# Three of four later taps of a causal convolution as a ScalarE product and a GpSimd add, in a fused attention-and-gate kernel on one core

## The chip, the cores and the metric

The kernel runs on one core of one Trainium2 chip. The metric is the device time of one execution in microseconds; the time before the change is the median of three runs, 591.73 us (590.05 to 592.37). Five engines work side by side, each through a queue of its own in the order in which the program gives it instructions: TensorE (PE, with its weight loads PEld), VectorE (DVE), ScalarE (ACT), GpSimd (POOL), and SyncE (SP), which here only issues DMAs. An engine whose next instruction waits for a semaphore holds up all that stands behind it in its queue.

## What is computed

Sigmoid attention over 8 batches of 12 heads, its result laid out as 768 features per token; then a gate (a causal convolution of five taps along the tokens, and a sigmoid), a product with `w_val`, the gate times that, and a product with `w_out`.

```python
def _attn_ref(q, k, v):                     # (8, 12, 448, 64) each
    scores = scale * np.matmul(q, k.transpose(0, 1, 3, 2)) - np.log(S)
    attn = 1.0 / (1.0 + np.exp(-scores))
    return np.matmul(attn, v).astype(np.float32)

def _moe_ref(x, w_val, conv_w, w_out):      # x: (8, 448, 768)
    xp = np.concatenate([np.zeros((B, K - 1, D), dtype=np.float32), x], axis=1)
    for k in range(K):                      # K = 5
        gate_pre += conv_w[k][None, None, :] * xp[:, k:k + S, :]
    gate = 1.0 / (1.0 + np.exp(-gate_pre))
    val = x @ w_val
    return (gate * val @ w_out).astype(np.float32)
```

## The kernel before

**Units.** Two heads make a pair (48, index `i`), two pairs a double pair (24, index `j`), three double pairs a batch. For a pair PE makes the scores of three chunks of 128 keys (`scores`, L496); the 64 keys that are left over are done for both pairs of a double pair at once (`scores_rest`, L518). ACT applies the sigmoid to each chunk (`attention`, L531). `attend` (L581, L589) multiplies with v into a bank of PSUM, and `after` copies that to `x`.

**Plain and split float32.** A plain pair multiplies float32 by float32 directly (`qk_single`, `a_single`). A split pair replaces each operand by a high and a low part and adds three faster products: `qk_hi` by a copy (L355 on DVE or L353 on ACT) and `qk_lo` by a subtraction on POOL (L364); `a` by a scaled copy on ACT (L359) and a DVE subtraction (L542), and `v_hi`, `v_lo`. `WHOLE_SCORES` lists the pairs with plain scores, `WHOLE` the double pairs with a plain attend.

**Convolution and products.** The first batch's attention output is cut into seven slices, one of which goes to each other batch: so seven batches of 512 tokens pass through gate and products. In `after`, for each of a double pair's two blocks of 128 features, the first tap is a scaled copy on ACT or DVE, and the four later taps are each one DVE instruction, `gate = x * w + gate` (L645); then ACT applies the sigmoid to the gate (L648). `x_scale` finds a batch's scale (with a small matmul, L665), `x_split` makes `xs` (L688), its high and low part. `product` (L707) makes one block of 128 output features from 18 matmuls of 512 columns: six blocks of input times three terms. The `val` products are taken out of PSUM by DVE (L717) and multiplied with the gate, the `out` products by ACT or DVE (`scaled`, L359 or L361), and go to the output in two DMAs (L725, L726). PSUM has three buffers for attention (`ps_a`) and two for products (`ps_m`).

**What sets the order.** Each piece of work is recorded by `op` with the engines that may do it, an assumed cost for each, a due time, and the buffers that it reads and writes. `Plan.issue` then simulates the engines once, before the program is built, and gives every engine the ready piece that is due first; a piece with two possible engines goes to the one that comes free. The due times come from the table `AT` and from `tau(i)`, which counts 8.2 for each of the first 12 pairs and 11.51 for the later ones. The plan keeps DVE and POOL from running together where both of their instructions carry `port="VG"`. Since the order is fixed when the program is built, a change of `AT` or of an assumed cost moves instructions in every queue.

**First loads.** A pair's q and k are one DMA of 896 columns (`load`, L459), v is one per double pair (`load_v`, L463), each weight column one of 768 KB (L402), all issued by SP.

## Time and profile before

| | |
|---|---|
| median of three runs | 591.73 us (590.05 to 592.37) |
| the profiled execution | 592.33 us; its span 590.5 us |
| instructions in the span | 9085 |
| bytes moved by DMA | 56.94 MB, 28.7% of the 16 DMA engines' span |
| granted TensorE clock | 1.00 throughout |

The profile is of one execution. Its page gives for each engine the time in which it worked, and a chain of waits followed back from the last instruction. Matmuls overlap: one of 512 columns is recorded with 379 ns, but the next begins 216 ns behind it. So a busy PE is best read by the distance from the start of one piece of work to the start of the next, in the timeline. The stages of the span are: loads until about 4 us; attention alone, with the conversion of the weights on DVE and ACT, until about 104 us; attention and products interleaved until about 500 us; and the last twelve products, some with nothing left beside them.

### The profile page before, as it was taken

To read this page: it belongs to the slowest core of one execution; us is meant where nothing else is said; L and a number is where in the kernel's file an instruction comes from. 1 tells how busy PE (TensorE), PEld (TensorE's weight loads), DVE (VectorE), ACT (ScalarE), POOL (GpSimd) and SP (SyncE) were. 2 spreads that over 40 slices of the span, in tenths; PEclk is the share of its full clock that TensorE was granted. 3 is DMA by queue.
4 is the path that set the end of the run, shared out by engine and by line. 5 is a ranking of instruction groups with operands and counts; after the bars stand their busy time and mean duration, and the time that the engine had idled before them with its cause. 6 is when DMAs were issued, how large, how long until landed. Compare 5 with 4: busy or idle time off the path is not lost. (4 is left out here: it accounts for less than half of the span.)

```text
span 590.5 us, 9085 instructions
## 1 busy us (share of the span) xinstructions
PE 578.1 (98%) x3503; PEld 273.4 (46%) x3503; DVE 463.4 (78%) x766; ACT 366.9 (62%) x478; POOL 70.5 (12%) x88
## 2 busy tenths in 40 slices
PE   8999999999999999999999999999999999999996
PEld 4333334444555445454454545545544455444442
DVE  0889999989999998989989899897982998722210
ACT  5678768566786767767776677676653875421111
POOL 0000202122111031111211111110011200000000
PEclk9999999999999999999999999999999999999999
DMA  8978622240423023231141411324004110021012
GB/s 322 382 276 275 223 95 65 66 117 18 130 72 109 11 84 130 81 101 62 32 130 47 134 63 33 99 72 139 1 34 158 37 42 1 1 71 37 1 36 72
DMA packets 30523, 56.94 MB, mean 96 GB/s; under 512 B 13968, under 2 KB 19344, under 8 KB 30480
## 3 DMA queue, kind: packets, MB, share of 16 engines
q1 hardware_dynamic: 30480, 56.37, 28.7%
q8 instruction: 27, 0.44, 0.3%
q14 instruction: 16, 0.13, 0.1%
HBM read 43.96 MB, written 12.40 MB: 95 GB/s over the span
## 5 line engine op out<-in xcount | busy, mean ns | idle before, releaser
L707 PE MATMUL ps_m<-g,w_out_hi 128*128 128x512 f16 x504 | 150.0, 379 | 1.3 <-ACT y L359 0.9
L707 PE MATMUL ps_m<-xs,w_val_hi 128*128 128x512 f16 x504 | 150.1, 379 | 0.6 <-DVE y L717 0.4
L645 DVE SCALAR_TENSOR_TENSOR gate<-x,cw,gate 128x512 f32<-128x512 f32 x168 | 121.8, 753 | 0.8
L364 POOL TENSOR_TENSOR qk_lo<-qk_src,qk_hi 128x448 fp32r<-128x448 f32 (+1 forms) x56 | 64.7, 1171 | 300.5 <-DVE qk_hi L355 111.3
L707 PE MATMUL ps_m<-xs,w_val_lo 128*128 128x512 f16 x252 | 95.5, 379 | 0.0
L707 PE MATMUL ps_m<-g,w_out_lo 128*128 128x512 f16 x252 | 95.5, 379 | 0.0
L542 DVE SCALAR_TENSOR_TENSOR a<-ps_a,a 128x896 f16<-128x896 f32 x84 | 89.0, 1082 | 4.8 <-ACT a L359 4.5
L531 ACT ACTIVATE ps_a<-ps_a 128x896 f32<-128x896 f32 x98 | 86.7, 906 | 8.6 <-DVE v_exp L523 7.8
L707 PEld LDWEIGHTS <-w_val_hi 128*128 128x128 f16 x504 | 47.9, 98 | 62.8 <-issue 7.8
L707 PEld LDWEIGHTS <-w_out_hi 128*128 128x128 f16 x504 | 48.0, 98 | 61.6 <-issue 6.3
L359 ACT ACTIVATE a<-ps_a 128x896 f16<-128x896 f32 x84 | 74.5, 924 | 0.3
L531 ACT ACTIVATE a_single<-ps_a 128x896 f32<-128x896 f32 x70 | 60.0, 922 | 7.2 <-PE ps_a L496 4.7
L359 ACT ACTIVATE y<-ps_m,o_scale 128x512 f32<-128x512 f32 x38 | 25.5, 686 | 60.6 <-PE ps_m L707 53.8
L717 DVE SCALAR_TENSOR_TENSOR y<-ps_m,y_scale,gate 128x512 f32<-128x512 f32 x42 | 29.9, 745 | 33.5 <-PE ps_m L707 33.5
L496 PE MATMUL ps_a<-qk_single 64*128 64x448 f32 x240 | 51.1, 555 | 2.2 <-DMA qk_single<-qk 1.4
L353 ACT CAST g<-y 128x512 f16<-128x512 f32 x33 | 20.5, 620 | 52.6 <-DVE y L717 52.2
L589 PE MATMUL ps_a<-a_single,v_src 128*64 128x448 f32 x240 | 47.3, 543 | 0.0
L589 PE MATMUL ps_a<-a,v_hi 128*64 128x448 f16 x336 | 46.1, 354 | 0.0
L648 ACT ACTIVATE gate<-gate 128x512 f32<-128x512 f32 x42 | 26.0, 627 | 28.9 <-DVE gate L645 28.7
L707 PEld LDWEIGHTS <-w_val_lo 128*128 128x128 f16 x252 | 24.7, 98 | 29.7
L707 PEld LDWEIGHTS <-w_out_lo 128*128 128x128 f16 x252 | 24.6, 98 | 29.8
L359 ACT ACTIVATE gate<-x,cw 128x512 f32<-128x512 f32 x32 | 23.1, 735 | 20.1 <-DVE y L717 20.1
(104 smaller groups left out, 658.4 us busy)
## 6 DMA issues: line engine op xcount, KB each, us to landing
qk_src<-qk SPq DMA_DIRECT2D x28, 448.0 KB, 3.7
v_src<-vs SPq DMA_DIRECT2D x24, 448.0 KB, 3.4
out_t<-y SPq DMA_DIRECT2D x42, 224.0 KB, 2.0
qk_single<-qk SPq DMA_DIRECT2D x20, 448.0 KB, 6.1
w_words<-w_val SPq DMA_DIRECT2D x6, 768.0 KB, 9.7
w_words<-w_out SPq DMA_DIRECT2D x6, 768.0 KB, 6.0
x<-first_x SPq DMA_DIRECT2D x21, 68.0 KB, 2.3
first_x<-x_first SPq DMA_DIRECT2D x3, 452.0 KB, 7.1
```

The costliest lines, as they stand in the source:

```text
L353: nc.scalar.copy(to, x)
L359: nc.scalar.activation(to, x, AF.Copy, scale=by)
L364: engines[eng].tensor_tensor(to, x, y, op=ALU.subtract)
L496: mm(b()[:, h, :S], k()[rows, at : at + P], q()[rows, :S], start=(n == 0), stop=(n == len(terms(i)) - 1))
L531: nc.scalar.activation(to, b()[:, :, :S], AF.Sigmoid, bias=-math.log(S), scale=1.0 / math.sqrt(D))
L542: op({"V": 1.0}, t + 0.5, lambda e: nc.vector.scalar_tensor_tensor(part(1), p(), A_SCALE, part(0), op0=ALU.mult, op1=ALU.subtract), [b], [ ...
L589: mm(px()[to, p, :S], v()[:, o : o + D], x(st[2 * j + p]["a", c])[:, h, at : at + S], start=False, stop=(c == 2 and n == len(parts) - 1), ...
L645: op({"V": 0.67}, at + AT["tap_step"] * k, lambda e, p=p, g=g, w=w, k=k: nc.vector.scalar_tensor_tensor(by(g()), x()[:, p, :, HALO - k : H ...
L648: op({"A": 0.55}, t + AT["gate"] + AT["tap_pair"] * p, lambda e, g=g: nc.scalar.activation(g(), g(), AF.Sigmoid), [], [g])
L707: mm(po(), w()[:, c, :], x(k), start=(c == 0 and j == 0), stop=(c == NC - 1 and j == 2))
L717: op({"V": 0.6}, t + AT["y"], lambda e: nc.vector.scalar_tensor_tensor(y(), po(), y_scale()[:, m : m + 1], gate(), op0=ALU.mult, op1=ALU.m ...
```

## The change

**The taps.** From the second batch on, three of the four later taps (`ADDED`; one of four in the first that has a gate, `ADDED_FIRST`) are no longer one DVE instruction each: ACT makes the product of `x` and the tap's weight into a new buffer, of which there are two (`tap_ring`), and POOL adds it to the gate. That is 114 of the 168.

```diff
-EARLY = 6
+EARLY = 5
+ADDED_FIRST = 1
+ADDED = 3
...
+    tap_ring = ring(sb, 2, [P, T], F32, "tap")
...
             for k in range(1, KT):
+                if k > KT - 1 - (ADDED_FIRST if f == 1 else ADDED):
+                    tap = tap_ring.new()
+                    op({"A": 0.61}, at + AT["tap_step"] * k - AT["tap_first"], lambda e, p=p, w=w, k=k, tap=tap: scaled(
+                        e, by(tap()), x()[:, p, :, HALO - k : HALO + SL - k], w(k)), [x, own, edge, cw], [tap])
+                    op({"G": 1.27}, at + AT["tap_step"] * k, lambda e, g=g, tap=tap: nc.gpsimd.tensor_tensor(
+                        g(), g(), tap(), op=ALU.add), [tap], [g])
+                    continue
                 op({"V": 0.67}, at + AT["tap_step"] * k, lambda e, p=p, g=g, w=w, k=k: nc.vector.scalar_tensor_tensor(
```

**Plain pairs.** Twenty pairs with plain scores become sixteen, ten double pairs with a plain attend nine.

```diff
-WHOLE = {*range(9), 21}
-WHOLE_SCORES = {*range(15), 17, 24, 39, 42, 43}
+WHOLE = {*range(8), 10}
+WHOLE_SCORES = {*range(15), 17}
```

**The first loads** get due times of their own, in the order of the pairs, and the very first is cut into 576 and 320 columns; chunk 0 of pair 0 waits only for the former.

```diff
+        x, t = s["qk"], t + AT["load_qk_first" if i < AHEAD else "load_qk"] if i >= 4 else -1e3 + i
+        if i:
+            op({"S": 0.45}, t, lambda e: nc.sync.dma_start(x(), qk[i]), [], [x], P * QW * 4)
+            return
+
+        s["more"] = more = x.part()
+        for n, (b, cs) in enumerate(((x, slice(0, S + P)), (more, slice(S + P, QW)))):
+            op({"S": 0.45}, t + 0.5 * n, lambda e, cs=cs: nc.sync.dma_start(
+                x()[:, cs], qk[i][:, cs]), [], [b], P * (cs.stop - cs.start) * 4)
...
-        op({"S": 0.45}, tau(2 * j) + AT["load_v"], lambda e: nc.sync.dma_start(v(), vs[j]), [], [v], P * VW * 4)
+        op({"S": 0.45}, tau(2 * j) + AT["load_v"] if j else -990, lambda e: nc.sync.dma_start(v(), vs[j]), [], [v], P * VW * 4)
...
-    def sources(i):
+    def sources(i, c=None):
+        if i == 0 and c != 0:
+            return [st[i]["qk"], st[i]["more"]]
```

SP's queue at the start of the program; `qk_single` is a pair's q and k, `v_src` a double pair's v. Before:

```order
L459 DMA qk_single_149<-qk 128x896
L463 DMA v_src_155<-vs 128x896
L459 DMA qk_single_157<-qk 128x896
L459 DMA qk_single_159<-qk 128x896
L463 DMA v_src_161<-vs 128x896
L459 DMA qk_single_163<-qk 128x896
L459 DMA qk_single_165<-qk 128x896
L402 DMA w_words_167<-w_val 128x768
```

SP's queue at the same place now:

```order
L471 DMA qk_single_149<-qk 128x576
L471 DMA qk_single_149<-qk 128x320
L466 DMA qk_single_156<-qk 128x896
L466 DMA qk_single_158<-qk 128x896
L466 DMA qk_single_160<-qk 128x896
L476 DMA v_src_162<-vs 128x896
L476 DMA v_src_164<-vs 128x896
L407 DMA w_words_166<-w_val 128x768
```

Both v loads stand behind four pairs; the first weight stands behind six loads' worth of bytes where there were seven.

**The last product** (block 5 of the last batch's `out`) is made as two of 256 columns, each with its own `ps_m` bank, eviction and DMA.

```diff
+        if (n, b, m) == ("out", B - 1, NC - 1):
+
+            y = y_ring.new()
+            for k, (low, cs) in enumerate(((y, slice(0, T // 2)), (y.part(), slice(T // 2, T)))):
+                po = columns(cs, t + k * STEP / 4)
+                op({"A": 0.35, "V": 0.4}, t + k * STEP / 4 + AT["o"], lambda e, cs=cs, po=po: scaled(
+                    e, y()[:, cs], po()[:, cs], outer[b]()[:, m : m + 1]), [po, outer[b]], [low], port="")
+                cs = slice(cs.start, min(cs.stop, S))
+                op({"S": 0.45}, t + k, lambda e, cs=cs: nc.sync.dma_start(out[b, m, :, cs], y()[:, cs]), [low], [], P * 1000)
+            op({"S": 0.45}, t + 2, lambda e: nc.sync.dma_start(out[0, m, :, S - SL :], y()[:, S:]), [low], [], P * 1000)
+            return
+        po = columns(slice(0, T), t)
```

`columns` holds the loop of 18 matmuls that stood in `product`, over a slice of columns.

**Due times and assumed costs.** Nearly every entry of `AT` has a new number, and some assumed costs too (POOL's 1.27 for `g_lo` is 1.17). Two entries:

```diff
-    first=8.2, step=11.51, val=-64.5, val_step=38.05, out=-42, out_step=46.57, w_max=-113, w_split=-46.5,
+    first=8.4, step=14.21, val=-51.5, val_step=42.5, out=-27, out_step=35.57, w_max=-84.5, w_split=-74,
```

What that moves on PE is seen where the first product begins. Before, behind the scores of pair 15 (the last row of `qk_lo` in each list is the last term of a chunk; the pair's first chunks are left out here):

```order
L496 MATMUL ps_a<-qk_lo,qk_hi 128x448 x2
L414 LDWEIGHTS ones
L414 MATMUL ps_m<-out_max,ones 128x1
L665 LDWEIGHTS ones
L665 MATMUL ps_m<-diagonal,ones 128x128
L518 MATMUL ps_a<-qk_src 64x448 x2
L518 MATMUL ps_a<-qk_single 64x448 x2
L581 MATMUL ps_a<-a_single,v_src 64x448 x4
L589 MATMUL ps_a<-a_single,v_src 64x448 x12
L496 MATMUL ps_a<-qk_hi 128x448 x2
L496 MATMUL ps_a<-qk_hi,qk_lo 128x448 x2
L496 MATMUL ps_a<-qk_lo,qk_hi 128x448 x2
```

Two more chunks of pair 16 follow there, and then the first product. PE's queue now, at the end of the same pair 15:

```order
L511 MATMUL ps_a<-qk_hi 128x448 x2
L511 MATMUL ps_a<-qk_hi,qk_lo 128x448 x2
L511 MATMUL ps_a<-qk_lo,qk_hi 128x448 x2
L731 LDWEIGHTS w_val_hi_73
L731 MATMUL ps_m<-xs,w_val_hi_73 128x512
```

The first product now stands directly behind pair 15; the rest, the attend and pair 16 come after the first two products.

In the middle of the program, ACT's queue (numbers tell the tiles apart; `tap` is the new buffer, `x` the convolution's input, `ps_a` a chunk of scores in PSUM). Before:

```order
L359 ACTIVATE a_2897<-ps_a_2852 128x2x448
L359 ACTIVATE gate_2907<-x_2465,cw_68 128x512
L359 ACTIVATE gate_2912<-x_2465,cw_68 128x512
L353 CAST g_2941<-y_2930 128x512
L531 ACTIVATE ps_a_2932<-ps_a_2932 128x2x448
L531 ACTIVATE ps_a_2943<-ps_a_2943 128x2x448
```

ACT's queue now, at the same double pair's first taps:

```order
L364 ACTIVATE tap_3033<-x_2565,cw_68 128x512
L364 ACTIVATE a_3039<-ps_a_2977 128x2x448
L364 ACTIVATE tap_3046<-x_2565,cw_68 128x512
L364 ACTIVATE tap_3062<-x_2565,cw_68 128x512
L364 ACTIVATE tap_3076<-x_2565,cw_68 128x512
L546 ACTIVATE ps_a_3066<-ps_a_3066 128x2x448
```

Two first taps stood between the scaled copy of one pair and the sigmoids of the next; now four products of later taps do, and the third and fourth of them need a buffer that POOL's add must have read before the sigmoid behind them can start.

## What is predicted

> **What bounds the kernel now.** I read the page's busy shares first, then the stages, then what TensorE waited for.
>
> ```profile
> PE 578.1 (98%) x3503; PEld 273.4 (46%) x3503; DVE 463.4 (78%) x766; ACT 366.9 (62%) x478; POOL 70.5 (12%) x88
> ```
>
> TensorE (PE) is busy for 98% of the span. The table of stages shows where the others stand (PE, weight loads, DVE, ACT, POOL, each with its busy us):
>
> ```profile
> 0.00:15.00 15.00, 12.23 (x86) 6.76 (x88) 0.76 (x3) 8.33 (x10) 0.89 (x11) 1.00 0.85 323
> 15.00:100.00 85.00, 82.37 (x475) 31.27 (x473) 79.72 (x160) 64.32 (x80) 6.72 (x7) 1.00 0.65 227
> 100.00:400.00 300.00, 299.45 (x1917) 149.15 (x1917) 277.65 (x440) 212.38 (x280) 52.43 (x59) 1.00 0.25 79
> ```
>
> From 100 to 400 us VectorE (DVE) is at 277.65/300 = 93%, ScalarE (ACT) at 71%, GpSimd (POOL) at 17%, and PE stands still for 0.55 us in all. DVE is nearly full but has not been the bound. A kernel like this gets faster by less PE work or by fewer PE waits. The waits are short; the longest three and the shortest of ten:
>
> ```profile
> PE ps_a L496 <- DMA qk_single<-qk: 1.4, 1, 1.4
> PE ps_m L707 <- ACT y L359: 1.1, 3, 0.8
> PE ps_m L740 <- DVE ones L733: 1.1, 1, 1.1
> ...
> PE ps_a L496 <- ACT a_single L531: 0.3, 1, 0.3
> ```
>
> All ten add up to 7.5 us; without the DMA row and the row of the warm-up's `ones`, 5.0 us are left that ACT and DVE could give back. So the relief of DVE, the largest part of the change in instructions, can be worth 5 us at the very most, and nothing for certain.
>
> **Plain or split pairs: less PE work.** `WHOLE_SCORES` goes from 20 pairs to 16, `WHOLE` from 10 double pairs to 9. The timeline of PE gives the price of each unit from the start of one piece to the start of the next. First a plain pair of scores and a plain attend:
>
> ```profile
> 111.94 2.53 PE L496 MATMUL ps_a<-qk_single 64*128 64x448 f32 x12
> 114.40 0.60 PE L707 MATMUL ps_m<-xs,w_val_hi 128*128 128x512 f16 x2
> ...
> 123.08 0.93 PE L581 MATMUL ps_a<-a_single,v_src 64*64 64x448 f32 x8
> 128.60 0.47 PE L496 MATMUL ps_a<-qk_hi 64*128 64x448 f32 x2
> ```
>
> Then the same in split form:
>
> ```profile
> 248.19 0.17 PE L515 MATMUL ps_a<-vm,ones 128*128 128x1 bf16 x1
> 248.28 0.98 PE L518 MATMUL ps_a<-qk_src 64*64 64x448 f32 x8
> 249.09 0.56 PE L581 MATMUL ps_a<-a_rest,v_hi 64*64 64x448 f16 x8
> ...
> 253.29 0.47 PE L496 MATMUL ps_a<-qk_hi 64*128 64x448 f32 x2
> ...
> 255.31 0.60 PE L707 MATMUL ps_m<-xs,w_val_hi 128*128 128x512 f16 x2
> ```
>
> Plain scores take 114.40 - 111.94 = 2.46 us, split ones 255.31 - 253.29 = 2.02: 0.44 less, four times, 1.76. A plain attend takes 128.60 - 123.08 = 5.52, a split one 253.29 - 249.09 = 4.20, and the extra `vm` matmul 0.09: 1.23 less, once. Together **-3.0 us** of PE work (2.6 to 3.4, by a tenth of a microsecond for each of the five units). The other engines pay for it: six more products of `a` on ACT and DVE, eight more halves of `qk_lo` on POOL, all beside PE's products.
>
> **The start: -1.7 us.** The timeline of all engines:
>
> ```profile
> 0.74 0.39 SPq L459 DMA_DIRECT2D qk_single<-qk  x1
> 1.18 0.42 SPq L463 DMA_DIRECT2D v_src<-vs  x1
> 4.27 2.53 PE L496 MATMUL ps_a<-qk_single 64*128 64x448 f32 x12
> 5.34 2.54 ACT L531 ACTIVATE a_single<-ps_a 128x896 f32<-128x896 f32 x3 [3.11 <-PE ps_a L496]
> 8.22 2.53 PE L496 MATMUL ps_a<-qk_single 64*128 64x448 f32 x12 [1.42 <-DMA qk_single<-qk]
> 12.72 0.98 PE L581 MATMUL ps_a<-a_single,v_src 64*64 64x448 f32 x8 [0.27 <-ACT a_single L531]
> ```
>
> The first scores need 576 of the 896 columns of the first load. At the 323 GB/s of the first stage a load of 448 KB takes 1.42 us (459 thousand bytes), so the 36% that are cut off are worth 0.5 us: first scores at 3.8 instead of 4.27. The second pair's load now stands ahead of the first v load, one load earlier, so about 1.4 us earlier than 8.2. Pair 0 ends at 6.3, so the wait of 1.42 goes nearly whole. What is late next is ACT: one sigmoid per 0.85 us (2.54/3), seven of them ahead of the first attend, from 4.9 to 10.8. The attend moves from 12.72 to about 11.0, hence 1.7; the bounds are 0.5 (only the shorter load counts) and 1.9. The first v load is now the sixth. With it 2.3 MB have passed, 7.1 us at 323 GB/s, behind 2.9 us of latency (4.27 less 1.42): there at about 10, in time. SP issues one DMA more, 0.4 us, before a queue that is not waited for.
>
> **The first products come earlier: +0.7 us.** PE's order now has the first product right behind pair 15; before, a rest, an attend and pair 16 stood in between.
>
> ```profile
> 95.53 0.18 PE L414 MATMUL ps_m<-out_max,ones 128*128 128x1 bf16 x1
> 102.04 0.47 PE L496 MATMUL ps_a<-qk_hi 64*128 64x448 f32 x2
> 104.07 0.61 PE L707 MATMUL ps_m<-xs,w_val_hi 128*128 128x512 f16 x2
> 101.83 2.17 DVE L688 SCALAR_TENSOR_TENSOR xs<-x,x_exp,xs 128x1024 f16<-128x1024 f32 x1
> ...
> L688 DVE SCALAR_TENSOR_TENSOR xs<-x,x_exp,xs 128x1024 f16<-128x1024 f32 x21 | 27.1, 1319 | 0.1
> ```
>
> That is 104.07 - 95.53 = 8.5 us earlier, 10.2 with the start. The third `xs` is first read after 24 of the 36 matmuls of two products, 5.2 us in (at the 0.217 us each that the chain of waits shows below): at 109.3 before, 99.1 now. DVE finished it at 104.0, with 5.3 us to spare. DVE's queue ahead of it is shorter by some 3.2 us (both orders priced with this trace's durations; mostly taps and part of a weight put behind it), and the first weights arrive one load, 1.4 us, earlier: ready at 99.4. The cover is gone, then, by 0.3 us. A row of 2.17 against a mean of 1.32 shows what one meeting with POOL costs here, 0.85, and POOL's first adds fall into this stage; I charge half of one more, 0.7 in all, with bounds of 0 and 4.9 (if DVE is not earlier at all).
>
> **The end: +0.3 us.** The chain of waits, then the timelines of ACT and SP:
>
> ```profile
> 577.18 0.69 ACT y L359
> ...
> 577.92 7.99 PE ps_m L707 x36
> 585.99 0.69 ACT y L359
> 586.95 0.41 SPq L725 DMA_DIRECT2D out_t<-y  x1
> ```
>
> The last product is cut in two halves of 256 columns. The first runs interleaved with product 4, as before; the second takes a `ps_m` bank that product 4 must leave first. Counted from 577.92: product 4's last matmul starts at 5.28 (the 36 took 7.99, 35 steps of 0.217 and a length of 0.38; half steps are 0.108), ACT starts 0.47 behind it and takes 0.69, so the second half starts at 6.5, though PE is free at 5.8. Its 18 matmuls end at about 8.7, its eviction (0.5, between nothing and 0.69) at 9.25, where 585.99 + 0.69 now stands at 8.76. SP was 0.27 late there (586.95 against 586.68) and no longer is. Net +0.2 to +0.5; bounds 0 and +0.8, because no row shows a matmul of 256 columns.
>
> **Taps from DVE to ACT and POOL: 0 on PE.** 114 of 168 taps leave DVE. One costs ACT a product and POOL an add. Rows by source line, and by group with busy us and mean ns:
>
> ```profile
> L645 DVE SCALAR_TENSOR_TENSOR gate<-x,cw,gate x168: 733/743/1618, 57.7 to 513.1; 128x512 f32<-128x512 f32 x168
> L359 ACT ACTIVATE gate<-x,cw 128x512 f32<-128x512 f32 x32 | 23.1, 735 | 20.1 <-DVE y L717 20.1
> L364 POOL TENSOR_TENSOR qk_lo<-qk_src,qk_hi x56: 987/1129/1995, 70.5 to 470.1; 128x448 fp32r<-128x448 f32 x28, 128x384 fp32r<-128x384 f32 x28
> L364 POOL TENSOR_TENSOR g<-y,g x2: 1161/1165/1169, 214.4 to 495.8; 128x512 f16<-128x512 f32 x2
> L542 DVE SCALAR_TENSOR_TENSOR a<-ps_a,a x84: 1074/1081/1092, 132.1 to 496.6; 128x896 f16<-128x896 f32 x84
> ...
> L364 DVE TENSOR_TENSOR g<-y,g 128x512 f16<-128x512 f32 x40 | 26.6, 685 | 0.8 <-ACT g L353 0.7
> L562 DVE SCALAR_TENSOR_TENSOR v_lo<-v_src,v_exp,v_hi 128x896 f16<-128x896 f32 x14 | 16.1, 1150 | 1.2
> ```
>
> 108 of them lie in some 405 us from 100 us on. DVE loses 108 x 0.725 (121.8/168) = 78 us, 19% of that stretch: 93% becomes 73%. ACT gains 108 x 0.72 (23.1/32) = 78 us: 71% becomes 90%, and 91% with 23 more `qk_hi` copies and 12 first taps fewer. No row shows a 128x512 float32 add on POOL; the nearest is 1.165 (bounds 0.99 and 2.0), so POOL gets 126 us, 17% becomes 49%. No engine is full, and DVE at 93% did not hold PE up, so I take 0 for ACT at 91%. Its bounds are -2.5 (half of the 5.0 us of waits goes) and +6 (the first rival).
>
> Where rows overlap POOL, a DVE tap once took 1618 ns against 743, while `a<-ps_a,a`, with one input in PSUM, stays within 1074 to 1092. The Trainium skill ("SBUF — State Buffer", section "Who interferes with whom") says that a DVE instruction with two SBUF inputs and a GpSimd instruction that reads SBUF exclude each other for their whole length, and this speaks against putting adds on GpSimd. Both rows agree. By that rule POOL's 49% and the two-input work left to DVE (54 taps, 39 us, with `xs`, `g` and `v_lo` 109 us, 27%) exclude each other, 76% together, and my sum stays.
>
> **Sum.** The profiled execution took 592.33 us (span 590.5 and 1.8 around it). -3.0 - 1.7 + 0.7 + 0.3 + 0 = -3.7 gives 588.6. The median of the runs, 591.73, lies 0.6 below that execution: **588.0 us**.
>
> **Rivals.** *ACT becomes the bound (slower).* The tap's product goes through two buffers, so the third in a row waits in ACT's queue for a POOL add, and behind it stand the sigmoids that free `ps_a` for PE. A group of six pairs takes about 73 us; 9% of it, 6.6 us, is ACT's slack. A late add costs 1995 - 1129 = 0.87 us; 18 adds belong to a group, so it decides from 8 late ones on; with ten, (8.7 - 6.6) x 6 groups = 13 us, 601, with nine 595. Against it: the median of 1129 says that most are not late. Chance 0.13, for 595 to 601.
>
> *DVE stands still during every add (slower).* 73% + 49% = 122%: PE would be held up by 22% of 405 us, 677. The lengthened tap (1618) speaks for it, the `a<-ps_a,a` row, never over 1092 in 84, against. Chance 0.02.
>
> *DVE holds the early stage (no change).* From 15 to 100 us DVE is at 79.72/85 = 94%. If its queue sets when the first product can run, the 1.7 us from the start only become a wait there, up to a microsecond more: 589.7 to 591. Chance 0.30.
>
> *The free DVE also gives back waits (faster).* Half of the 5.0 us: 585.5. Chance 0.13.
>
> That the tap's move does nothing for the time is no rival but my forecast; the gain is in the pairs and the start. Forecast 587 to 589.3: chance 0.42.
>
> **How the numbers follow.** Half a per cent is 3 us, about what a measurement can tell (the three runs span 590.05 to 592.37), so "faster" means under 588.8 us. Three quarters of the forecast lie there (0.32), the give-back rival (0.13) and some of the early-stage one (0.06): 0.51. Slower is ACT's and the standstill's: 0.15. The rest, 0.34, is no change. The range goes from 584.5 (the give-back and the wider start) to 594.5 (the wider first product, or eight to nine late adds).
>
> **What would show it.** Plain `qk_single` rows fall from 240 to 192, and the waits on `qk_single<-qk` by DMA go; first attend near 11.0; a wait before or inside the first product on `xs`, none if its DVE row ends before 99; a pause of 0.7 ahead of the last 18 matmuls; ACT near 90%, DVE near 73% between 100 and 400 us, with PE at 299 of 300. Wrong would be PE waits on ACT in that stretch, a row of POOL adds well over 1.2 us, or DVE taps near 1.6.

## The result, and the profile after

The changed kernel takes **596.25 us** (median of 6 runs, 595.81 to 596.76) against 591.79 for the kernel before (6 runs): ratio 1.0079, 95% interval 1.0065 to 1.0093. It is slower by 4.5 us; 588.0 was forecast, and the range ended at 594.5. The profiled execution has a span of 594.2 us, where it was 590.5.

The page's busy shares, then the stages of 100 to 400 us and 400 to 525 us (PE, weight loads, DVE, ACT, POOL in busy us):

```profile
PE 578.1 (97%) x3562; PEld 277.0 (47%) x3562; DVE 445.6 (75%) x674; ACT 435.7 (73%) x598; POOL 242.5 (41%) x212
```

```profile
100.00:400.00 300.00, 295.16 (x1904) 146.57 (x1903) 252.21 (x352) 251.73 (x353) 170.87 (x143) 1.00 0.26 80
400.00:525.00 125.00, 123.61 (x798) 61.60 (x797) 97.73 (x138) 95.36 (x134) 61.65 (x50) 1.00 0.16 49
```

PE stood still for 0.55 us between 100 and 400 us; now it does for 300 - 295.16 = 4.84, and for 1.39 more up to 525. ACT is at 84% there, not at the forecast 91%, and DVE at 252.21/300 = 84%, not at 73%. The table of PE's waits over the whole span says for whom (us in total, times, longest):

```profile
PE ps_a L511 <- DVE a_rest L557: 3.0, 5, 1.1
PE ps_a L533 <- ACT a_single L546: 2.1, 4, 0.9
PE ps_m L731 <- DVE y L755: 1.8, 5, 0.8
...
PE ps_a L511 <- DVE x L360: 0.6, 1, 0.6
```

New at the top is `a_rest`: the scores of a later pair want a PSUM bank that DVE has not emptied yet. Three of these four rows name DVE, the engine that was relieved; the waits of the other row, for ACT, lie in the first 100 us. The groups of instructions by line (busy us, mean ns of one, then idle time ahead of them) show what became of it:

```profile
L664 POOL TENSOR_TENSOR gate<-gate,tap 128x512 f32<-128x512 f32 x114 | 161.3, 1418 | 126.6 <-DVE gate L667 89.8 <-ACT tap L364 29.3 <-DVE vm L525 3.0
...
L557 DVE SCALAR_TENSOR_TENSOR a<-ps_a,a 128x896 f16<-128x896 f32 x90 | 95.0, 1080 | 13.2 <-ACT a L364 13.1
L667 DVE SCALAR_TENSOR_TENSOR gate<-x,cw,gate 128x512 f32<-128x512 f32 x54 | 45.7, 856 | 0.1
L369 DVE TENSOR_TENSOR g<-y,g 128x512 f16<-128x512 f32 x38 | 30.8, 823 | 3.5 <-ACT g L358 3.4
...
L360 DVE CAST g<-y 128x512 f16<-128x512 f32 x20 | 11.3, 578 | 0.0
...
L670 ACT ACTIVATE gate<-gate 128x512 f32<-128x512 f32 x42 | 26.3, 625 | 7.3 <-POOL gate L664 7.3
```

An add takes 1.42 us, where 1.165 was taken. A DVE tap went from a mean of 753 to 856 ns and a subtraction `g` from 685 to 823, while `a<-ps_a,a`, with an input in PSUM, stays at 1080. ACT's sigmoids of the gate wait 7.3 us for POOL's adds. One place where DVE is late, 199 to 207 us, in the timeline (start, length, engine, instruction, then the idle time ahead and what ended it):

```profile
201.40 2.36 DVE L369 TENSOR_TENSOR g<-y,g 128x512 f16<-128x512 f32 x2
201.62 3.27 POOL L664 TENSOR_TENSOR gate<-gate,tap 128x512 f32<-128x512 f32 x2 [0.98 <-DVE gate L667]
...
203.69 0.15 DVE L538 TENSOR_SCALAR v_exp<-ps_a 128x1 int32<-128x1 int32 x1
...
203.87 0.90 ACT L546 ACTIVATE ps_a<-ps_a 128x896 f32<-128x896 f32 x1 [1.24 <-DVE v_exp L538]
...
204.80 0.92 ACT L364 ACTIVATE a_rest<-ps_a 128x896 f16<-128x896 f32 x1
...
205.75 1.09 DVE L557 SCALAR_TENSOR_TENSOR a_rest<-ps_a,a_rest 128x896 f16<-128x896 f32 x1 [1.73 <-ACT a_rest L364]
...
206.90 0.47 PE L511 MATMUL ps_a<-qk_hi 64*128 64x448 f32 x2 [1.06 <-DVE a_rest L557]
```

Read from the end: PE waits 1.06 us for `a_rest` on DVE, that for ACT's copy, that for ACT's sigmoid, and that (1.24 us) for a tiny `v_exp` on DVE, which stood behind two subtractions. Those take 2.36 us together, where twice the mean of the kernel before is 1.37, beside two adds that take 3.27. The hypothesis of all that follows: the adds and DVE keep each other out of SBUF, DVE loses time, and short instructions behind it that release PE come late.

### The profile page after: what moved, and what is told of

Same layout as the page of the kernel before. It is cut to its first block, busy times and chain, and to the rows that moved or that the text cites. A ratio compares the mean times of both kernels' runs of the same rounds, so it can differ in the third digit from the quotient of the medians.

```text
span 594.2 us, 9495 instructions
## 1 busy us (share of the span) xinstructions
PE 578.1 (97%) x3562; PEld 277.0 (47%) x3562; DVE 445.6 (75%) x674; ACT 435.7 (73%) x598; POOL 242.5 (41%) x212
## 4 chain that ended last, share of the span: by engine, by line
PE 45%; DVE 31%; ACT 12%; issue 7%; POOL 2%; DMA 1%; DVEq 0%; ACTq 0%; POOLq 0%
PE ps_m L731 31%; DVE a L557 6%; PE ps_a L511 6%; PE ps_a L604 6%; ACT ps_a L546 3%; DVE gate L667 3%; DVE y L755 2%; ACT a L364 2%; POOL gate L664 2%; DVE gate L366 2%; DVE xs L710 2%; ACT a_single L546 1%; DMA v_src<-vs 1%; DVE x_max L647 1%; DVE a_rest L557 1%
## 5 line engine op out<-in xcount | busy, mean ns | idle before, releaser
L664 POOL TENSOR_TENSOR gate<-gate,tap 128x512 f32<-128x512 f32 x114 | 161.3, 1418 | 126.6 <-DVE gate L667 89.8
L731 PE MATMUL ps_m<-g,w_out_hi 128*128 128x512 f16 (+1 forms) x516 | 150.4, 374 | 2.6 <-DVE y L755 1.0
L369 POOL TENSOR_TENSOR qk_lo<-qk_src,qk_hi 128x448 fp32r<-128x448 f32 x64 | 74.4, 1180 | 74.9 <-ACT qk_hi L358 40.2
L364 ACT ACTIVATE tap<-x,cw 128x512 f32<-128x512 f32 x114 | 81.0, 730 | 23.0 <-POOL gate L664 22.4
L731 PE MATMUL ps_m<-g,w_out_lo 128*128 128x512 f16 (+1 forms) x258 | 96.5, 374 | 0.0
L364 ACT ACTIVATE y<-ps_m,o_scale 128x512 f32<-128x512 f32 (+1 forms) x36 | 23.7, 683 | 40.2 <-PE ps_m L731 39.4
L667 DVE SCALAR_TENSOR_TENSOR gate<-x,cw,gate 128x512 f32<-128x512 f32 x54 | 45.7, 856 | 0.1
L511 PE MATMUL ps_a<-qk_hi 64*128 64x448 f32 x192 | 40.0, 413 | 4.2 <-DVE a_rest L557 3.0
L358 ACT CAST g<-y 128x512 f16<-128x512 f32 x22 | 13.5, 614 | 40.3 <-DVE y L755 39.9
L511 PE MATMUL ps_a<-qk_single 64*128 64x448 f32 x192 | 40.8, 557 | 0.8 <-DVE a L557 0.4
```

The source lines that it names most:

```text
L358: nc.scalar.copy(to, x)
L364: nc.scalar.activation(to, x, AF.Copy, scale=by)
L369: engines[eng].tensor_tensor(to, x, y, op=ALU.subtract)
L511: mm(b()[:, h, :S], k()[rows, at : at + P], q()[rows, :S], start=(n == 0), stop=(n == len(terms(i)) - 1))
L664: op({"G": 1.27}, at + AT["tap_step"] * k, lambda e, g=g, tap=tap: nc.gpsimd.tensor_tensor(g(), g(), tap(), op=ALU.add), [tap], [g])
L667: op({"V": 0.67}, at + AT["tap_step"] * k, lambda e, p=p, g=g, w=w, k=k: nc.vector.scalar_tensor_tensor(by(g()), x()[:, p, :, HALO - k : H ...
```

## The experiments

The kernel before took 591.77 to 592.33 us beside these runs; the ratios are to it. So the times of two sets of runs can differ by half a microsecond for no other reason. Where "same order" is said, the planner's order of all queues is kept, and only what an instruction does is changed. The letters of the theories hold within one expectation.

### The adds, shortened and replaced

**e1**, same order, adds over 8 of 512 columns:

```diff
-                        g(), g(), tap(), op=ALU.add), [tap], [g])
+                        g()[:, :8], g()[:, :8], tap()[:, :8], op=ALU.add), [tap], [g])
```

> The changed kernel with every one of the 114 GpSimd adds cut to 8 of its 512 columns (the convolution leaves out those taps in the other columns); all four compute queues keep their order. Theory A (the adds: 1.42 us each on GpSimd, and VectorE instructions with two SBUF inputs shut out meanwhile, make VectorE and through it the scores late): the PE waits between 100 and 525 us, 6.2 us in the changed kernel, fall below 1.5 us and the time to 589 to 591.5 us. Theory B (the order that the new due times make is bad by itself): the waits stay, 594.5 us or more.

Measured: **587.52 us**, ratio 0.9919 (0.9904 to 0.9933). Its busy shares, its stage from 100 to 400 us, and groups by line:

```profile
PE 575.4 (98%) x3562; PEld 277.6 (47%) x3562; DVE 417.0 (71%) x674; ACT 435.4 (74%) x598; POOL 119.5 (20%) x212
```

```profile
100.00:400.00 300.00, 299.28 (x1953) 149.81 (x1952) 238.23 (x361) 256.54 (x360) 85.44 (x146) 1.00 0.26 81
```

```profile
L667 DVE SCALAR_TENSOR_TENSOR gate<-x,cw,gate 128x512 f32<-128x512 f32 x54 | 40.9, 768 | 0.4 <-ACT gate L364 0.2
...
L369 DVE TENSOR_TENSOR g<-y,g 128x512 f16<-128x512 f32 x38 | 25.6, 685 | 2.6 <-ACT g L358 2.5
...
L664 POOL TENSOR_TENSOR gate<-gate,tap 128x8 f32<-128x8 f32 x114 | 36.1, 317 | 181.7 <-DVE gate L667 96.5 <-ACT tap L364 80.4 <-DVE a L557 2.8
```

With the same instructions on DVE, 28.6 us of its time are gone (445.6 to 417.0), PE stands still for 0.72 us from 100 to 400 us, and the time is below theory A's range and 0.5 below the forecast. The rest of the change brings at least what was forecast; the length of the adds costs 8.7 us (9.3 by the differences to the kernel before in each set of runs, 4.5 and 4.8).

**Where the 8.7 us are paid.** In both kernels PE has the same instructions in the same order, so their two profiles can be laid side by side, start by start. From 100 us on, PE in the changed kernel falls 8.8 us behind e1, 7.6 of them at these places. For each, the chain of waits in the changed kernel was followed back to the instructions that ran longer than in e1:

| PE at (us) | falls behind by (us) | the chain leads back to |
|---|---|---|
| 110.4, 141.0, 206.9 | 0.77, 0.84, 1.07 | a DVE tap of 1.76 us, one of 1.66, a subtraction `g` of 1.76, each beside adds |
| 282.1 to 283.1, 358.4 to 359.4, 434.7 to 435.7 | 0.91, 1.09, 1.14 | a DVE first tap of 1.49 us and the subtraction behind it, 1.75, beside adds |
| 294.0, 370.3, 446.6 | 0.21, 0.21, 0.19 | DVE instructions of 1.50 and 1.12 us, beside adds and beside a subtraction `qk_lo` on POOL |
| 307.8, 384.1, 460.4 | 0.21, 0.23, 0.22 | ACT's sigmoid of the gate, which waits 1.03 us for POOL's adds |
| 509.3 | 0.55 | a DVE first tap of 1.57 us and, behind it, a POOL add that ACT's next tap waits for |

So 6.4 of these 7.6 us come by DVE instructions that ran about 1 us longer beside POOL, 0.7 by gates that come late through POOL, and the last place by both. The waits that the profile names add up to less than this slip: at 110.4 us PE's next matmul starts 0.97 us behind the last one where e1 has 0.20, but only 0.61 us are recorded as idle.

**e2**, same order; POOL fills the tap buffer instead, 1536 columns so that it takes as long (1.41 us), reading nothing; the adding is left out:

```diff
-    tap_ring = ring(sb, 2, [P, T], F32, "tap")
+    tap_ring = ring(sb, 2, [P, 3 * T], F32, "tap")
...
-                    ... nc.gpsimd.tensor_tensor(
-                        g(), g(), tap(), op=ALU.add), [tap], [g])
+                    ... nc.gpsimd.memset(
+                        tap(), 0.0), [tap], [g])
```

> The changed kernel with every add replaced by a GpSimd memset of 1536 columns of the tap buffer, which occupies GpSimd about as long but reads nothing from SBUF (the three taps are left out of the convolution). Theory A1 (exclusion of VectorE's two-input work by a GpSimd instruction that reads): VectorE's gate taps return to 0.74 us, the time falls as in the run with short adds, 589 to 591.5. Theory A2 (GpSimd's occupation alone: ScalarE's products wait for the two buffers and hold up the sigmoids behind them): 594.5 or more, as in the changed kernel, provided that the memset takes 1.2 us or more.

Measured: **595.94 us**, 1.0068 (1.0047 to 1.0089); DVE busy 442.7. It is as slow as with the adds, though the taps are back at 0.75 us as theory A1 said: other instructions are held:

```profile
L667 DVE SCALAR_TENSOR_TENSOR gate<-x,cw,gate 128x512 f32<-128x512 f32 x54 | 39.9, 751 | 0.1
...
L369 DVE TENSOR_TENSOR g<-y,g 128x512 f16<-128x512 f32 x38 | 26.5, 708 | 3.5 <-ACT g L358 3.4
...
L366 DVE TENSOR_SCALAR gate<-x,cw 128x512 f32<-128x512 f32 x22 | 24.9, 1133 | 0.0
L360 DVE CAST g<-y 128x512 f16<-128x512 f32 x20 | 21.2, 1074 | 0.0
...
L670 ACT ACTIVATE gate<-gate 128x512 f32<-128x512 f32 x42 | 26.3, 626 | 0.0
```

The two-input instructions are free again (751, 708). The cast `g`, 424 ns beside short adds and 578 beside full ones, takes 1074. So POOL's writing alone holds DVE's casts and scales, and the two-input ones are held only where POOL reads. The Trainium skill ("SBUF — State Buffer", section "Who interferes with whom") says just this: copies, casts and scales in a two-port mode contend with any GpSimd instruction, two-input ones only with its reads. The prediction used the second half alone.

e2 also bears on the gates: no gate waits for a fill, so ACT's sigmoid of the gate never waits for POOL here (last row), and the time is the same. So a price of this size needs no late gates. PE falls behind e1 mostly at the same places as in the table above, from 280 to 447 us.

### Was it ACT, waiting for a tap buffer?

**e5**, same order, six tap buffers instead of two:

```diff
     tap_ring = ring(sb, 2, [P, T], F32, "tap")
+    tap_ring.make = lambda: sb.tile([P, T], F32, name="tap", bufs=6)
```

> The changed kernel with six tap buffers in place of two; every queue keeps its order, so ScalarE's products no longer wait for GpSimd's adds (22.4 us of such waits in the changed kernel). Theory A2 (those waits hold up the sigmoids, and so PE): the time falls by 3 to 8 us, to 588 to 593 us. Theory A1 (GpSimd's adds and VectorE's instructions exclude each other, and VectorE's queue hands the delay on): within 1 us of the changed kernel, 595.3 to 597.3, with PE's waits on VectorE's a_rest as before.

Measured: **596.18 us**, 1.0069 (1.0054 to 1.0084), as with two, though ACT's products no longer wait for POOL (22.4 us before). The prediction's first rival, ACT held by two tap buffers, is not what costs the time.

### DVE's time by itself

**e10** and **e14** keep the 8-column adds and put idle work into DVE's queue: ahead of each tap and each subtraction `g`, 92 times, a multiplication of 220 (e10) or 88 (e14) columns.

```diff
+    held = lambda: nc.vector.tensor_scalar(idle(), idle(), warm[:, :1], None, op0=ALU.mult)
...
+        if eng == "V":
+            held()
...
-                ... lambda e, p=p, g=g, w=w, k=k: nc.vector.scalar_tensor_tensor(
+                ... lambda e, p=p, g=g, w=w, k=k: held() and nc.vector.scalar_tensor_tensor(
```

> The changed kernel with adds of 8 of 512 columns (the rest of those products is left out) and the same order, and ahead of each VectorE tap (54) and each VectorE subtraction g (38) one idle VectorE multiplication of 220 columns, estimated at 0.31 us from 0.63 us for 512 columns: VectorE gets back some 28 us of time without work and GpSimd gets none. Theory A1 (VectorE's lost time alone is the price; that the gates come later through longer adds is not): 593 to 597. Rival A2 (the adds' own length in the chain of the gates is the price, VectorE's lost time is hidden): 587.5 to 589. Both in part: between.

> As the run with idle VectorE multiplications behind 8-column adds (594.65), but with 88 columns instead of 220, estimated at 0.18 us each from 0.377 us at 220; 92 of them are some 16 us of VectorE time. Theory A4 with slack (the price grows with VectorE's load, slowly at first): 588.5 to 590.5, like the 1.5 us that 10.9 us of held time cost. Theory of one price per us of VectorE's time (0.28 us for 1): 591.5 to 592.5.

Measured: e10 **594.65**, 1.0048 (1.0034 to 1.0061); e14 **592.30**, 1.0006 (0.9997 to 1.0015). The idle work took longer than estimated (rows of e10, then of e14):

```profile
L332 DVE TENSOR_SCALAR idle<-idle,warm 128x220 f32<-128x220 f32 x92 | 34.7, 377 | 0.0
```

```profile
L332 DVE TENSOR_SCALAR idle<-idle,warm 128x88 f32<-128x88 f32 x92 | 28.2, 307 | 0.0
```

So time taken from DVE with short adds on POOL costs up to 7.1 us (587.52 to 594.65); the number is in theory A1's range, but it does not bear theory A1 out. Laid beside e1 as above, e10 falls behind by 5.0 us up to 116 us, 2.1 of them in one wait on `x` (as in e14). Then 1.7 come by PE's clock:

```profile
100.00:400.00 300.00, 294.94 (x1904) 147.56 (x1902) 249.71 (x412) 250.78 (x353) 85.96 (x143) 0.99 0.25 80
```

The granted clock is 0.66 from 115 to 120 us, and matmuls of 512 columns start 0.43 us apart there (0.22 in e1); in the changed kernel the clock is 1.00. Behind 213 us, where 57 of the 92 idle instructions lie and take 21.6 us of DVE's time, e10 loses 0.1 us; the changed kernel loses 5.9 there. So e10 and e14 do not price the adds: DVE's lost time, here in pieces of 0.38 us, can cost PE nothing. e14's 592.30 lies in the range of its second theory, but with 28.2 us of idle work instead of 16 it does not bear that out either.

**e9**, same order, adds over 256 columns:

```diff
-                        g(), g(), tap(), op=ALU.add), [tap], [g])
+                        g()[:, :256], g()[:, :256], tap()[:, :256], op=ALU.add), [tap], [g])
```

> The changed kernel with the same order in every queue; each GpSimd add covers 256 of the 512 columns, the other half of those products is left out. The adds took 1.42 us each at 512 columns and 0.32 at 8, so here some 0.8. Theory A (each add holds VectorE for a time that grows with the add's length, and the held time reaches the PE): about halfway between 587.5 (8 columns) and 596.2 (512), 590.5 to 592.5, and VectorE busy about 431 us between 417.0 and 445.6. Rival B (VectorE has slack for short holds, and only the longest cost time): 587.5 to 589.5, although VectorE's busy time is halfway.

Measured: **589.00**, 0.9954 (0.9941 to 0.9966); adds of 0.85 us, DVE busy 427.9. This is in rival B's range: 10.9 us of DVE's time, 38% of the 28.6, cost only 1.5.

**e13**, same order, the whole work, each add cut into two of 256 columns; and **e17**, the same with nothing waiting for the result:

```diff
-                        g(), g(), tap(), op=ALU.add), [tap], [g])
+    e13:  [... g()[:, h : h + 256], g()[:, h : h + 256], tap()[:, h : h + 256] ... for h in (0, 256)]
+    e17:  [... spare()[:, h : h + 256], tap()[:, h : h + 256], tap()[:, h : h + 256] ... for h in (0, 256)]
```

> The changed kernel, all of its work, the same order; each GpSimd add is two adds of 256 columns, one behind the other. An add of 256 columns took 0.85 us by itself, so a pair takes some 1.5 to 1.7 against 1.42 of the whole. Theory A3 (the length of one hold counts: the VectorE instruction between waits for half an add, not for a whole one): 590 to 594. Rival A4 (the sum of the holds counts): 596 to 599, since the sum is as large or larger.

> As the run with adds in two pieces (595.94), but each piece adds the product to itself into a spare tile: the adding of the three taps to the gate is left out, GpSimd's time stays the same, and neither the next tap nor the sigmoid waits for it. Theory A5 (the rest of the price is that gates come late through GpSimd): VectorE busy 432 to 438, time 590.5 to 593. Rival A4 (the hold alone): 595 to 597 at the same VectorE time.

Measured: e13 **595.94**, 1.0063 (1.0048 to 1.0078); e17 **588.61**, 0.9950 (0.9936 to 0.9963). The groups of e13, then of e17:

```profile
L664 POOL TENSOR_TENSOR gate<-gate,tap 128x256 f32<-128x256 f32 x228 | 184.2, 836 | 112.9 <-DVE gate L667 85.4 <-ACT tap L364 23.8 <-DVE a L557 2.8
...
L670 ACT ACTIVATE gate<-gate 128x512 f32<-128x512 f32 x42 | 26.4, 628 | 12.7 <-POOL gate L664 11.3 <-POOL x L645 1.0
```

```profile
L665 POOL TENSOR_TENSOR spare<-tap 128x256 f32<-128x256 f32 x228 | 156.2, 713 | 81.4 <-ACT tap L365 81.0
...
L671 ACT ACTIVATE gate<-gate 128x512 f32<-128x512 f32 x42 | 26.3, 625 | 0.0
```

Shorter pieces do not help: the time lies between the ranges of A3 and A4. In e13 the pair takes 2 x 0.836 = 1.67 us, and though DVE is held for only 18.1 us, the time is the same. ACT's sigmoids of the gate wait 11.3 us for POOL. The three places of the table above that go by the sigmoid cost 0.65 us each here instead of some 0.22. Without that dependence 588.61 is left, below the expectation of theory A5; but DVE's busy time (429.1 against 435.1) and POOL's fell with it, so e17 does not part the two cleanly. What all these runs say, by the time that DVE's busy time stands above e1's 417.0, and the time above 587.52:

| run | DVE, us more | time, us more |
|---|---|---|
| e9, adds of 256 columns | 10.9 | 1.5 |
| e17, two halves, not waited for | 12.1 | 1.1 |
| e13, two halves | 18.1 | 8.4 |
| e14, idle work on DVE | 20.5 | 4.8 |
| e10, idle work on DVE | 25.1 | 7.1 |
| e2, fills | 25.7 | 8.4 |
| the changed kernel | 28.6 | 8.7 |

Except for e13 the price rises with DVE's lost time, slowly at first, but that is no price for a microsecond: e10 and e14 lose their time at other places than the adds do, and e13 loses more of it by late gates. In the changed kernel the table of places gives late gates 0.7 us, and 0.55 in part.

### The chain that PE waits on

**e12**, only DVE's queue: `v_exp` ahead of the subtractions that stand directly before it, in two places (one with a single subtraction, and the one of 201 us).

```diff
-TENSOR_TENSOR g<-y,g 128x512
-TENSOR_TENSOR g<-y,g 128x512
 TENSOR_SCALAR v_exp<-ps_a 128x1
+TENSOR_TENSOR g<-y,g 128x512
+TENSOR_TENSOR g<-y,g 128x512
```

> The changed kernel; in VectorE's queue alone two v_exp instructions are moved ahead of the g subtractions that stood directly before them (one place with one of them, one with two). Theory A says that the chain held subtractions, v_exp, ScalarE's sigmoid of the rest, the last eviction of the rest, PE is how the loss reaches PE at such places: the second place loses up to 2.4 us of wait there, of which PE got 1.06; the time falls by 0.5 to 1.5, to 594.7 to 595.7. If PE is held by something else: 596.0 to 596.5.

Measured: **595.13**, 1.0055 (1.0043 to 1.0068): 1.1 us less. The same place in its timeline:

```profile
201.64 2.37 DVE L369 TENSOR_TENSOR g<-y,g 128x512 f16<-128x512 f32 x2
...
201.80 3.35 POOL L665 TENSOR_TENSOR gate<-gate,tap 128x512 f32<-128x512 f32 x2 [1.02 <-DVE v_exp L538]
...
203.64 0.92 ACT L364 ACTIVATE a_rest<-ps_a 128x896 f16<-128x896 f32 x1
...
204.59 1.09 DVE L558 SCALAR_TENSOR_TENSOR a_rest<-ps_a,a_rest 128x896 f16<-128x896 f32 x1 [0.52 <-ACT a_rest L364]
```

The subtractions are held just as long, but `a_rest` is evicted at 204.59 instead of 205.75, and PE's 1.06 us there are gone. The chain read above is the path at that place.

### Less or more on POOL

**e11**, same order: of the three taps one (k = 2) is a DVE instruction again where its add stood, 36 times (the expectation counts 38). **e15**, same order: the subtractions `g` of DVE go to POOL; **e16**: only those of the odd products.

```diff
-    nc.gpsimd.tensor_tensor(g(), g(), tap(), op=ALU.add)
+    e11, k == 2:  nc.vector.scalar_tensor_tensor(by(g()), x()[...], w(k), by(g()), op0=ALU.mult, op1=ALU.add)
-    lambda e: sub(e, g()[:, 1, :], y(), g()[:, 0, :])
+    e15:  sub("G", ...)
+    e16:  sub("G" if m % 2 else e, ...)
```

> The changed kernel; of the three later taps that ScalarE and GpSimd share, one (k = 2) is a VectorE instruction again, put where its add stood, so every other instruction keeps its place. VectorE gains 38 taps of about 0.75 us (28.5 us) and loses a third of the 28.6 us of held time; ScalarE loses 38 products. Theory A (the price is paid on VectorE): VectorE's time rises by some 19 us net, so the time rises above 596.2, by up to as much as the 28.6 us of held time cost (8.7 us): 598 to 605. Rival C (the hold itself is what hurts, ordinary VectorE work in its place is planned for): 592 to 595.

> The changed kernel, all of its work; the 38 g subtractions in VectorE's queue are issued by GpSimd, at the same places of the one issue order. VectorE loses 30.8 us of work; 38 more GpSimd instructions of about 1.3 us hold it for some 9 us at the measured 0.25 us for each. Theory A (VectorE's time is the price, 0.3 us for 1): net -21 us of VectorE's time, 589 to 592. Rival D (the subtraction now waits behind the taps' adds in GpSimd's queue, g comes late and the products wait for it, or the qk_lo behind it come late): 597 to 606.

> As the run before it, for the odd ones of the six products alone: some 19 subtractions go to GpSimd, VectorE loses 15 us and is held 5 us more. Theory A: 592 to 594.5. Rival D: 596.5 to 601.

Measured: e11 **598.52**, 1.0116 (1.0101 to 1.0131); e15 **592.98**, 1.0011 (1.0003 to 1.0020); e16 **589.52**, 0.9958 (0.9942 to 0.9975). The shares of e11, e15 and e16:

```profile
PE 579.2 (97%) x3562; PEld 277.2 (46%) x3562; DVE 465.9 (78%) x710; ACT 414.4 (69%) x562; POOL 194.6 (33%) x176
```

```profile
PE 576.5 (98%) x3562; PEld 277.1 (47%) x3562; DVE 419.2 (71%) x636; ACT 436.4 (74%) x598; POOL 286.6 (49%) x250
```

```profile
PE 575.4 (98%) x3562; PEld 277.4 (47%) x3562; DVE 427.9 (73%) x655; ACT 436.3 (74%) x598; POOL 264.8 (45%) x231
```

Fewer adds with more work on DVE are worse: in e11 DVE has 20 us more and the time rises by 2.3. Taking 19 subtractions from DVE gives 6.7 us back, more than the 1.7 to 4.2 expected, though POOL has more to do and holds DVE's taps longer; **e16 beats both kernels**, with the whole computation. Taking all 38 gives DVE its lowest load of these and loses 3.5 of it again, between its two expectations: relief for DVE is not all that counts. In e15's trace PE falls behind e1 by 1.6 us at 155.8, 207.3, 381.3 and 456.8 us, where ACT waits for POOL's adds, in a queue of POOL that is fuller now.

**e18**, e16 with the order of e12:

> The changed kernel, all of its work; the g subtractions of the odd products on GpSimd (589.52) and v_exp ahead of the subtractions directly before it in VectorE's queue. With only 0.2 us of PE's waits for the last eviction of the rest left, there is little to win: 588.7 to 589.6. If the two are independent and add up (1.1 us): 588.2 to 588.6.

Measured: **589.36**, 0.9962 (0.9949 to 0.9974). The two do not add up: with DVE relieved, the place that e12 mends no longer waits.

### Parts of the change, planned anew

In these the planner made its order anew, with due times (`AT`) that belong to another plan: **e3**, the changed kernel with all taps on DVE; **e6**, with two of three taps moved; and the kernel before, its own due times kept, with only the taps (**e4**), only the pair sets (**e7**) or only the first loads (**e8**).

```diff
-ADDED_FIRST = 1
-ADDED = 3
+e3: ADDED_FIRST = 0, ADDED = 0        e6: ADDED_FIRST = 1, ADDED = 2
 the kernel before, e7:
-WHOLE = {*range(9), 21}
-WHOLE_SCORES = {*range(15), 17, 24, 39, 42, 43}
+WHOLE = {*range(8), 10}
+WHOLE_SCORES = {*range(15), 17}
```

> The changed kernel with all 168 later taps back on VectorE, all else (due times, loads, pairs, split product) as changed; the plan is made anew. Theory A: the gain in the pairs and the start shows, 587.5 to 590.5 us. Theory B: 594 us or more.

> The changed kernel with two of four later taps moved in place of three (78 adds instead of 114; the plan is made anew with the changed due times). If the price is one per add (596.25 with 114, 587.5 with adds cut short), a third fewer adds give 593 to 594.5 us. If the due times were fitted to three taps (628.8 with none), the order is worse and the time 598 us or more.

> The kernel before with the taps alone moved as in the change (ScalarE's product due 5 units ahead of GpSimd's add), its own due times, pairs and loads. Theory A: slower by 4 to 8 us, 596 to 600 us. Theory B: 590.5 to 593 us.

> The kernel before with the changed sets of plain pairs alone, its own due times. By the PE work of the prediction (3.0 us less) 588.5 to 589.8 us, if no new waits come; if the old due times were fitted to the old sets, PE waits take it back: 591 to 597 us.

> The kernel before with the changed first loads alone. If the early stage is bound by PE, the 1.3 us by which the first attend moved in the changed kernel show: 590.3 to 591.2 us. If VectorE holds the stage up to the first product, it becomes a wait there: 591.8 to 593 us.

| run | us | ratio (95%) |
|---|---|---|
| e3, no taps moved | 628.79 | 1.0615 (1.0592 to 1.0639) |
| e6, two taps moved | 610.43 | 1.0311 (1.0293 to 1.0328) |
| e4, taps alone | 611.45 | 1.0322 (1.0297 to 1.0346) |
| e7, pairs alone | 611.88 | 1.0329 (1.0310 to 1.0348) |
| e8, first loads alone | 608.15 | 1.0269 (1.0252 to 1.0287) |

Every one is 16 to 37 us slower than the kernel before, even e8, which moves only five loads and splits one of them; the times of e4, e7 and e8 lie outside all that was expected. The granted clock is lower too, 0.978 to 0.996, where the kernel before has 0.998 to 1.00. They don't price the parts: what they show is that the due times fit one plan, and that each of these edits, by letting the planner choose again, costs far more than the part is worth. Only the runs that keep the order answer the question.

## Why the prediction was wrong

**The step that failed: "Taps from DVE to ACT and POOL: 0 on PE".** It cost 8.7 us (e1). Three things in it were wrong:

- "76% together, and my sum stays" took the exclusion for a question of average shares. Two engines below 100% together still meet, and a meeting lengthens one of the two instructions: with a median of 741 ns, single DVE taps took up to 1755, and with a median of 1282, single adds up to 2212. Over 114 adds DVE lost 28.6 us. The price was then set by a dozen places where such an instruction stood ahead of what PE waited for.
- The 27% of two-input work left out casts and scales, which POOL holds as well (e2: 424 to 1074 ns for the cast `g`). The section of the Trainium skill that was named says so too, and the trace agrees.
- DVE was never to be at 73%. In e1, with adds of 8 columns, it is at 238.23/300 = 79%. The planner had also moved other work to it, which the step did not charge, as these rows of the kernel before and of e1 show:

```profile
L361 DVE TENSOR_SCALAR gate<-x,cw 128x512 f32<-128x512 f32 x10 | 4.8, 476 | 0.0
```

```profile
L366 DVE TENSOR_SCALAR gate<-x,cw 128x512 f32<-128x512 f32 x22 | 18.5, 842 | 0.0
```

That is 13.7 us more for first taps alone: 5.7 for twelve more of them at 476 ns, and 8.0 because nine of the 22 stand beside subtractions `qk_lo` on POOL in e1 and take 1.22 to 1.42 us. And "DVE at 93% did not hold PE up" did not carry over. In the new order PE stands still for 4.84 us with DVE at 84% from 100 to 400 us, and for 1.62 and 2.02 with DVE at 82% (e9, e16). That the order before had its late DVE work where PE did not need it is likely, but was not tried.

**The rivals.** The slower end came, but not by a rival that was priced. ACT's tap buffers (0.13) are refuted by e5. The standstill (0.02) came nearest, with a wrong price: "PE would be held up by 22%" took all of DVE's work as excluded; 28.6 us of hold cost 8.7. The early stage did not hold (below), and the free DVE gave nothing back. Of the signs named for an error, "a row of POOL adds well over 1.2 us" is there; the one at 1.6 us for a DVE tap shows only in single taps (up to 1755 ns); their mean of 856 looks harmless. "PE waits on ACT in that stretch" is not there: the table's rows of 100 to 525 us name DVE alone.

**Less PE work, -3.0: consistent, but not measured by itself.** The timeline has a plain pair of scores at 78.59 - 76.13 = 2.46 us, as before, and the group of plain scores has 192 matmuls, where there were 240:

```profile
76.13 2.53 PE L511 MATMUL ps_a<-qk_single 64*128 64x448 f32 x12
78.59 0.20 PE L419 MATMUL ps_m<-out_max,ones 128*128 128x1 bf16 x2
```

```profile
L511 PE MATMUL ps_a<-qk_single 64*128 64x448 f32 x192 | 40.8, 557 | 0.8 <-DVE a L557 0.4 <-ACT a_single L546 0.4
```

**The start, -1.7: -1.3.** The timeline:

```profile
1.08 3.38 PE L778 MATMUL ps_m<-ones 128*128 128x128 bf16 x30 [1.08 <-DVE ones L771]
...
4.40 4.95 PE L511 MATMUL ps_a<-qk_single 64*128 64x448 f32 x24
...
11.46 0.98 PE L596 MATMUL ps_a<-a_single,v_src 64*64 64x448 f32 x8 [0.46 <-ACT a_single L546]
```

The second pair no longer waits for its load, and ACT is what is late next, as forecast. But the first scores start at 4.40, not at 3.8 (4.27 before). They did not wait for the load, which landed 2.9 us behind its issue (3.0 before), at 3.7: ahead of them in PE's queue stand 30 warm-up matmuls, which run until 1.08 + 3.38 = 4.46 (4.33 before). So the prediction took the wrong wait, and the attend comes at 11.46 instead of about 11.0.

**First products earlier, +0.7: 0.** The first product starts at 94.08, 10.0 earlier, as forecast (10.2). The third `xs`:

```profile
94.08 0.60 PE L731 MATMUL ps_m<-xs,w_val_hi 128*128 128x512 f16 x2
...
97.97 1.28 DVE L710 SCALAR_TENSOR_TENSOR xs<-x,x_exp,xs 128x1024 f16<-128x1024 f32 x1
...
99.27 0.59 PE L731 MATMUL ps_m<-xs,w_val_hi 128*128 128x512 f16 x2
```

It was ready at 99.25 (99.4 forecast), and PE read it at 99.27 without a wait. The cover is gone as was said, but the charge for one meeting with POOL was not due.

**The end, +0.3: -0.3.** From the last pair of products on (581.96):

```profile
588.52 0.38 PE L731 MATMUL ps_m<-g,w_out_hi 128*128 128x256 f16 x2 [0.50 <-ACT y L364]
...
590.73 0.47 ACT L364 ACTIVATE y<-ps_m,o_scale 128x256 f32<-128x256 f32 x1 [2.26 <-PE ps_m L731]
591.23 0.33 SPq L745 DMA_DIRECT2D out_t<-y  x1
```

The second half starts 6.56 after the pair and its eviction ends at 9.24; 6.5 and 9.25 were forecast. The span ends 594.2 - 581.96 = 12.24 after the pair's start, where it was 590.5 - 577.92 = 12.58. The mistake lies behind the eviction: 3.0 us follow it instead of 3.8, and only 0.3 of that (SP's lateness) was counted. That the last transfers are shorter is the likely rest; it was not tried.

With -3.0 (as forecast), -1.3, 0 and -0.3 the change without the adds' price is worth -4.6; e1 gives -4.8 (592.33 to 587.52). The forecast for the same terms was -3.7: the first products and the end came out better, the start worse. The failed step alone turns the sign.

## What to carry to other kernels

When work moves to GpSimd, price what its SBUF accesses do to VectorE's casts, scales and two-input instructions, not only the two engines' shares; then look in VectorE's queue for instructions behind the held ones that release TensorE. The sum of the lost time is no price: 21.6 us of idle work cost 0.1 us behind 213 us in e10, and some 1.1 us lost at 202 us in the changed kernel cost 1.07. Where the planner's order hangs on fitted due times, test a part with the order frozen, and count what the new plan moved onto the relieved engine. And ask whether the engine that was relieved has other work to give away: here 19 subtractions on GpSimd turned +4.5 us into -2.5.

## What was unexpected of the hardware

A GpSimd fill that reads nothing held VectorE's casts more than adds did (1074 against 578 ns), for the order here. A float32 add on GpSimd took 0.32 us for 8 columns, 0.85 for 256 and 1.42 for 512 beside VectorE's work, with medians of 0.20, 0.73 and 1.28. On VectorE a scale in SBUF of 88 columns took 307 ns and one of 220 took 377: cutting it shorter saves little. In e10 the granted clock fell to 0.66 from 115 to 120 us, behind 5 us in which PE was busy for 2.68 us; in e14, with 3.00 us there, it stayed at 1.00.
